# Retention and MoE kernel: two scalings moved to GpSimd, attention steps regrouped in the first GEMM2, and the last output tile copied by two engines

## The chip, the cores and the metric

The kernel runs on one core of one Trainium2 chip. The metric is the device time of one execution in microseconds (us); lower is better. The engines of the core are named as the profile names them: PE (TensorE, matmuls; PEld is its weight load), DVE (VectorE), ACT (ScalarE), POOL (GpSimd) and SP (SyncE, which here only issues DMAs).

## The reference

A causal retention layer (attention without softmax, with a decay per head) is followed by a two-layer network with a hardswish gate.

```python
# q, k, v: (8 batches, 8 heads, 576 positions, 64), w_in: (512, 2048), w_out: (2048, 512)
scores = scale * np.matmul(q, k.transpose(0, 1, 3, 2))
gamma = 1.0 - 2.0 ** (-5.0 - np.arange(H))
Dmat = np.where(rel >= 0, gamma[:, None, None] ** rel, 0.0)      # rel = pos[:, None] - pos[None, :]
attn = np.matmul(scores * Dmat, v)                               # x = attn as (4608, 512)
h = x @ w_in
g = h * np.clip(h + 3.0, 0.0, 6.0) / 6.0
out = g @ w_out                                                  # (4608, 512) float32
```

## The kernel before

**Pieces and blocks.** The 576 positions of a batch are cut into four pieces of 128 ("main") and a rest of 64; rests of two batches share a piece. Pieces 0 to 3 give the 512 tokens of block 0, pieces 4 to 7 those of block 1, and so on; block 8 holds all rests. For a piece the kernel loads K (`kn`) and Q with V (`qv`) from HBM through GpSimd's DMA queue (`load`, three DMAs each, with a cast to float16; six buffers), scales V, and in blocks from 2 on Q too, by the decay (`vs`), transposes K and Q (`qk`), forms scores, masks them (`at`), multiplies by V and adds what the state of earlier pieces contributes (`intra`, `inter`, `state_mm`); the result, cast, is the input `xt` of the network. `update_mm` and `update_state` carry the state on.

**Two ways to transpose.** For pieces 0 to 7, TensorE transposes K and Q into PSUM (`k_by_pe`, `q_by_pe`) and ScalarE copies them out. From piece 8 on, SyncE issues a transposing DMA for K (`transpose_k`) and, after Q and V have been scaled by one instruction over 128x1024, one for Q (`transpose_q`). `ahead(c)` does both for piece c.

**The network.** GEMM1 of a block is 16 units (`g1`) of four matmuls; ScalarE and VectorE form the gate (`gt`, lines 423 and 424). GEMM2 of block 0 is 16 units of four matmuls, (tile, part), `g2`; GEMM2 of later blocks uses seven products of half-size matrices (`product` 1 to 7, line 533) instead of eight. It needs differences of quarters of W_out (`combine_wout` 1 to 4, tiles `tw`) and sums of quarters of the gate (`sum_of`, tiles `s`, line 507). `gather` puts the products together and stores them.

**Order.** The order on each engine is written out by hand: instructions are issued engine by engine in the order of the program, and each waits for its own operands. `put(units, steps)` issues a list of units, and behind unit j the steps listed under j; `run_later` issues masks that were put off. In GEMM2 of block 0 the units go part by part over tiles 0 to 2, then tile 3. `first_step(c)` behind a unit finishes piece c-1, transposes piece c+1, forms the scores of piece c and scales V of piece c. In GEMM1 of block 1 the steps are the transposing DMAs and scalings of pieces 8 to 11. `seven_block(kb, mine, next_)` is GEMM2 of block kb with the attention of two blocks around it: pieces `mine` (c0 to c3) are finished, and the pieces `next_` (n0 to n3) are prepared. In block 1, `ahead(n0)` and `ahead(n1)` (pieces 12 and 13) stand behind product 2 and `gather(kb, 2)`; their scores come under `begin(n0, n1)`, just ahead of product 4.

**Resources.** PSUM has the tag `ph` with four banks (gates, units, transpositions), and `sc` (two banks), `tu` and `o` (one bank each).

Of the kernel before, what the change touches and what calls it, by code (L numbers as in the profile page):

```python
# [10 lines left out]
FP32 = mybir.dt.float32  # L11
FP16 = mybir.dt.float16
ACTF = mybir.ActivationFunctionType
ALU = mybir.AluOpType
# [3 lines left out]
def kernel(  # L18
# [16 lines left out]
    nc = tc.nc  # L35
# [3 lines left out]
    P = 128  # L39
# [50 lines left out]
    loaded = {}  # L90
# [144 lines left out]
            nc.tensor.transpose(pk[:, p, :], kn[:, 2 * p:2 * p + 2, :], ident16)  # L235
        nc.scalar.copy(qk_of(c)[:, 1], pk)

    def q_by_pe(c):
        q16, qk = loaded[c]["q16"], qk_of(c)
        pq = psum.tile([P, NPAIR, P], FP32, tag="ph", bufs=4, name=f"trq_{c}")  # L240
        for p in range(NPAIR):
            for h2 in range(2):
                r = slice(h2 * HALF, h2 * HALF + HALF)
                nc.tensor.matmul(pq[r, p, :], q16[:, 2 * p + h2, :], dq[:, 2 * p + h2, :],
                                 start=(p == 0), stop=(p == NPAIR - 1), skip_group_check=True)
        if c == EARLY - 1:
            for p in (0, 2):
                nc.scalar.copy(qk[:, 0, p:p + 2], pq[:, p:p + 2])
        else:
            nc.scalar.copy(qk[:, 0], pq)  # L250
# [54 lines left out]
    def transpose_k(c):  # L305
        nc.sync.dma_start_transpose(qk_of(c)[:, 1], loaded[c]["kn"].rearrange("s h d -> s (h d)"))

    def transpose_q(c):
        vs = work.tile([P, 2, H, D], FP16, tag="vs", bufs=6, name=f"vs_{c}")
        st[c]["vs"] = vs[:, 1]  # L310
        nc.vector.tensor_tensor(out=vs, in0=loaded[c]["qv"], in1=gqv, op=ALU.mult)  # L311
        nc.sync.dma_start_transpose(st[c]["qk"][:, 0], vs[:, 0].rearrange("s h d -> s (h d)"))

    def scores(c, late=9, given=False):
# [67 lines left out]
    def update_state(c):  # L382
        kind, b, i, _ = pieces[c]
        if kind == "rest":
            return
        u = st[c]["u"]
        scale = gc_b[1 if i == PER - 1 and b % 2 else 0]
        tag, bufs = ("tf", B) if i == PER - 1 else ("ts", 4)
        ts = work.tile([P, NPAIR, D], FP16, tag=tag, bufs=bufs, name=f"ts_{c}")
        if i == 0:  # L390
            nc.vector.tensor_tensor(out=ts, in0=u, in1=scale, op=ALU.mult)
        else:
            ta = work.tile([P, NPAIR, D], FP32, tag="ta", bufs=2, name=f"ta_{c}")
            nc.vector.tensor_tensor(out=ta, in0=u, in1=state_of[b], op=ALU.add)
            nc.vector.tensor_tensor(out=ts, in0=ta, in1=scale, op=ALU.mult)
            st[c].setdefault("before", state_of[b])
        state_of[b] = ts
# [162 lines left out]
    def last_block(kb):  # L560

        my = seven[kb] = {}
        for i, q1 in done_to[kb].items():
            sum_of(kb, i, q1, 8)

        def both(which):
            for tt in range(2):
                product(kb, which, tt)

        def keep(which):  # L570
            my[which] = work.tile([P, 2, half_n], FP32, tag=f"part{which}", bufs=1,
                                  name=f"part{which}_{kb}")
            for tt in range(2):
                nc.scalar.copy(my[which][:, tt], my["b"][tt])

        both(1)
        keep(1)
        both(2)
        gather(kb, 2)
        store_rest(0, 2, lo_n, my["lo"][:, :, lo_n], (nc.sync, nc.sync))  # L580
        sum_of(kb, 4, 0, 8)
        sum_of(kb, 3, 0, 8)
        both(5)
        gather(kb, 5)
        both(6)
        keep(6)
        both(3)
        ends = {name: work.tile([P, 2, half_n], FP32, tag=f"end{name}", bufs=1,
                                name=f"end{name}_{kb}") for name in ("c12", "c22", "c21")}
        nc.vector.tensor_tensor(out=ends["c12"], in0=my[6], in1=my["c_all"], op=ALU.add)  # L590
        store_rest(0, 2, hi_n, ends["c12"], (nc.sync, nc.sync))
        for tt in range(2):
            product(kb, 7, tt)
            nc.vector.tensor_tensor(out=ends["c22"][:, tt], in0=my[5][:, tt], in1=my["b"][tt],
                                    op=ALU.add)
        store_rest(2, 2, hi_n, ends["c22"], (nc.sync, nc.scalar))
        for tt in range(2):
            product(kb, 4, tt)
            nc.scalar.copy(ends["c21"][:, tt], my["b"][tt])
            store_rest(2 + tt, 1, lo_n, ends["c21"][:, tt:tt + 1], (nc.sync, nc.scalar))  # L600

    def store2(kb, i, src):
# [55 lines left out]
    def unit2(kb, mc, part):  # L658
        return lambda: g2(kb, mc, part)

    def first_step(c):


        old, new, b = c - 1 >= EARLY, c + 1 < 8, pieces[c - 1][1]
        if old:
            before = state_of.get(b)
            o = psum.tile([P, NPAIR, P], FP32, tag="o", name=f"o_{c - 1}")
            st[c - 1].update(o=o, first=True)
            copy = intra(c - 1, copy_later=True, more=before is not None)
            update_mm([c - 1])  # L670
            load_until(c - 1 + NBUF)
            update_state(c - 1)
        if new:
            q_by_pe(c + 1)
        if old and new:
            run_later(9)
        if EARLY <= c < 8:
            scores(c, 0)
        if old and before is not None:
            state_mm(o, before, st[c - 1]["qk"], slice(0, P), False, True)  # L680
        if new:
            k_by_pe(c + 1, "ph" if old else "tu")
        if old:
            copy()
        if c < 8:
            run_later(9)
        if EARLY <= c < 8:
            scale_v(c)

    def ahead(c):  # L690
        transpose_k(c)
        transpose_q(c)

    def scores_second(c, tags):

# [33 lines left out]
    def seven_block(kb, mine, next_):  # L729

        seven[kb] = {}
        c0, c1, c2, c3 = mine
        n0, n1, n2, n3 = next_ or [None] * 4

        def both(which):
            for tt in range(2):
                product(kb, which, tt)

        def begin(one, other, tags):
            update_mm([one, other])  # L740
            masks[one] = scores(one, given=True)
            masks[other] = scores_second(other, tags)

        def mask(c):
            masks.pop(c)()

        def done(*cs):
            for c in cs:
                loaded.pop(c)

        run_later(9)
        for i, q1 in done_to[kb].items():
            sum_of(kb, i, q1, 8)
        if kb == SEVEN:
            begin(c0, c1, ("ph", "ph"))
            load_until(c1 + NBUF)
        both(1)
        gather(kb, 1)
        if kb == SEVEN:
            mask(c0)  # L760
        update_state(c0)
        spread_state(c0)
        if kb == SEVEN:
            mask(c1)
        elif next_:
            ahead(n0)
            ahead(n1)
        both(2)
        if kb == SEVEN:
            update_state(c1)  # L770
        gather(kb, 2)
        if kb == SEVEN:
            ahead(n0)
            ahead(n1)
        else:
            update_state(c1)
        both(6)
        gather(kb, 6)
        inter(c0)
        inter(c1, "ph")  # L780
        intra(c0)
        intra(c1)
        spread_state(c1)
        begin(c2, c3, ("ph", "ph"))
        done(c0, c1)
        load_until(c3 + NBUF)
        sum_of(kb, 3, 0, 8)
        mask(c2)
        sum_of(kb, 4, 0, 8)
        both(5)  # L790
        gather(kb, 5)
        update_state(c2)
        spread_state(c2)
        mask(c3)
        both(7)
        gather(kb, 7)
        update_state(c3)
        both(3)
        gather(kb, 3)
        inter(c2, "ph")  # L800
        inter(c3, "ph")
        intra(c2)
        intra(c3)
        done(c2, c3)
        if next_:
            begin(n0, n1, ("ph", "o"))
            load_until(n1 + NBUF)
            ahead(n2)
            ahead(n3)
            mask(n0)  # L810
            mask(n1)
        both(4)
        gather(kb, 4)
# [7 lines left out]
    def gemm1(kb, steps, at_units):  # L821
# [8 lines left out]
        for j, (i, q0, q1) in zip(at_units, early_sums):  # L830
# [5 lines left out]

    load_until(EARLY - 1 + NBUF)
    gemm1(0, {9: [(fill_gq,)]}, ())
    order = [(mc, part) for part in range(4) for mc in range(3)] + [(3, part) for part in range(4)]
    steps = {3: [(first_step, 3)], 6: [(make_mask_rest,)], 9: [(first_step, 4)],  # L840
             11: [(first_step, 5)], 13: [(first_step, 6)],
             14: [(first_step, 7), (transpose_k, 8)], 15: [(transpose_k, 9)]}
    for j, i in zip((5, 6, 7, 8), (1, 2, 3, 4)):
        steps.setdefault(j, []).append((combine_wout, i))
    put([unit2(0, mc, part) for mc, part in order], steps)

# [6 lines left out]
    for fc, cols in ((2, done), (0, last), (1, last), (3, done), (2, last), (3, last)):  # L853
        g1_columns(1, fc, banks[fc], cols)
    gts.pop(0)


    gemm1(1, {0: [(transpose_q, 9)], 1: [(transpose_k, 10)],
              4: [(transpose_q, 10)], 5: [(transpose_k, 11)], 8: [(transpose_q, 11)]}, (2, 6))
    spare += tbd[0:PER - 1]  # L860
    for kb in range(1, NMB - 1):
        seven_block(kb, of_block(kb + 1), of_block(kb + 2))
# [33 lines left out]
```

## Time and profile before

| | |
|---|---|
| time, median of 3 runs | 300.46 us (298.76 to 301.93) |
| the profiled execution | 300.89 us, span of its instructions 299.1 us |
| PE busy | 286.1 us (96%) |
| DVE busy | 233.4 us (78%) |
| ACT busy | 181.4 us (61%) |
| POOL busy | 109.0 us (36%) |
| instructions | 6608 |

In the rows of the timeline the first number is the start in us from the first instruction, the second the length; then engine, line, operation, tiles written and read, and in brackets the idle time before it and what ended it. In rows of windows stand the stretch, its length, the busy time of PE, PEld, DVE, ACT and POOL with the number of instructions, the granted clock of TensorE as a share, the share of time that the DMA engines were in use (it can exceed 1, since waiting packets count) and GB/s. Rows of DMA issues end with the KB of one and the median us from issue to landing. A group of the page ends with busy time, mean ns of one, and idle time before it. A "q" behind an engine's name is its queue of DMA issues.

### The profile page before, as it was taken

The numbers are of one execution on the slowest core, as the hardware profiler recorded it, in microseconds if no ns is written. First come the engines' busy times: TensorE is split into PE (matmuls) and PEld (weight loads), VectorE is DVE, ScalarE is ACT, GpSimd is POOL, SyncE is SP. The second block draws the span as 40 slices with busy tenths as digits, with TensorE's granted clock in tenths as the row PEclk, the third lists the DMA queues.
The fourth block names the chain that finished last, engine by engine and source line by source line (L and its number), as shares of the span: only waits on it lengthen the run. The fifth ranks groups of instructions, "written<-read, shape, count | busy, mean of one in ns | idle before, by whom it ended". The sixth has DMA issues, their size and how long they took to land.

```text
span 299.1 us, 6608 instructions
## 1 busy us (share of the span) xinstructions
PE 286.1 (96%) x2646; PEld 185.7 (62%) x2646; DVE 233.4 (78%) x386; ACT 181.4 (61%) x311; POOL 109.0 (36%) x135
## 2 busy tenths in 40 slices
PE   7889998999969999999999999999999999999994
PEld 2644445547844488548854884488448844884583
DVE  4758656799965999699969996999699979637951
ACT  5558535585636856785677567755785577427720
POOL 8982567736770007501750175019720000000000
PEclk9999999999998999999999999999999999999998
DMA  9999999999999619991999299929992250011014
GB/s 71 149 184 206 189 162 216 168 122 150 141 202 154 94 37 145 169 149 35 160 153 148 42 154 151 148 39 127 156 177 52 77 139 0 2 72 70 3 35 106
DMA packets 153327, 35.56 MB, mean 119 GB/s; under 512 B 143568, under 2 KB 149200, under 8 KB 153296
## 3 DMA queue, kind: packets, MB, share of 16 engines
q0 software_dynamic: 117264, 18.36, 93.8%
q1 hardware_dynamic: 35728, 16.52, 28.5%
q8 instruction: 20, 0.33, 0.5%
q10 hardware_dynamic: 304, 0.26, 0.3%
q14 instruction: 11, 0.09, 0.1%
HBM read 36.70 MB, written 9.44 MB: 154 GB/s over the span
## 4 chain that ended last, share of the span: by engine, by line
PE 75%; DMA 11%; DVE 6%; POOL 4%; issue 1%; ACT 1%; ACTq 0%; DVEq 0%; POOLq 0%
PE ph L416 36%; PE b L533 17%; PE c L533 8%; DMA wout<-in_moe_w_out_dram 5%; PE a L533 4%; DMA win<-in_moe_w_in_dram 3%; PE o L353 3%; POOL qv L101 2%; DMA qk<-vs 2%; PE sc L321 1%; POOL kn L101 1%; DVE s L507 1%; DVE tw L492 1%; PE o L204 1%; DVE at L325 1%
## 5 line engine op out<-in xcount | busy, mean ns | idle before, releaser
L424 DVE SCALAR_TENSOR_TENSOR gt<-u,ph 128x512 f16<-128x512 f32 x144 | 97.4, 686 | 31.2 <-ACT u L423 29.2
L423 ACT ACTIVATE u<-ph,cb 128x512 f32<-128x512 f32 x144 | 98.6, 688 | 27.1 <-PE ph L416 26.4
L416 PE MATMUL ph<-xt,win 128*128 128x512 f16 x496 | 109.4, 382 | 0.5 <-ACT xt L287 0.4
L416 PEld LDWEIGHTS <-win 128*128 128x128 f16 x560 | 55.1, 98 | 65.7 <-issue 2.0
L101 POOL DMA_DIRECT2D kn<-in_k_dram x40 | 34.4, 867 | 97.9 <-PE u L377 91.1
L533 PEld LDWEIGHTS <-s 128*128 128x128 f16 x512 | 49.4, 98 | 6.5 <-DVE s L507 0.2
L533 PEld LDWEIGHTS <-gt 128*128 128x128 f16 x384 | 36.6, 98 | 7.6 <-DVE gt L424 1.1
L101 POOL DMA_DIRECT2D qv<-in_q_dram x40 | 34.4, 868 | 5.9 <-DMA wout<-in_moe_w_out_dram 3.4
L101 POOL DMA_DIRECT2D qv<-in_v_dram x40 | 34.7, 873 | 3.0 <-DMA wout<-in_moe_w_out_dram 1.6
L533 PE MATMUL b<-tw,s 128*128 128x256 f16 x256 | 30.6, 273 | 0.0
L359 ACT CAST xt<-o 128x512 f16<-128x512 f32 x31 | 17.0, 590 | 16.4 <-PE o L353 13.4
L325 DVE TENSOR_TENSOR at<-sc,mask_wide 128x1024 f16<-128x1024 f32 x19 | 23.2, 1222 | 1.7 <-PE sc L321 1.5
L507 DVE TENSOR_TENSOR s<-gt 128x512 f16<-128x512 f16 (+2 forms) x39 | 23.1, 591 | 0.3
L543 ACT COPY part<-b 128x512 f32<-128x512 f32 x14 | 8.2, 587 | 18.6 <-PE b L533 18.6
L311 DVE TENSOR_TENSOR vs<-qv,gqv 128x1024 f16<-128x1024 f16 x28 | 18.2, 685 | 0.0
L708 ACT CAST raw<-sc 128x512 f16<-128x512 f32 x28 | 15.1, 593 | 3.6 <-PE sc L702 3.4
L533 PE MATMUL b<-tw,gt 128*128 128x256 f16 x128 | 16.0, 280 | 0.0
L533 PE MATMUL b<-wout,gt 128*128 128x256 f16 x128 | 15.6, 273 | 0.0
L533 PE MATMUL c<-tw,s 128*128 128x256 f16 x128 | 15.4, 273 | 0.0
L533 PE MATMUL c<-wout,s 128*128 128x256 f16 x128 | 15.3, 273 | 0.0
L533 PE MATMUL a<-wout,gt 128*128 128x256 f16 x128 | 15.3, 273 | 0.0
L474 PE MATMUL pout<-wout,gt 128*128 128x512 f16 x64 | 14.8, 379 | 0.0
(93 smaller groups left out, 262.3 us busy)
## 6 DMA issues: line engine op xcount, KB each, us to landing
kn<-in_k_dram POOLq DMA_DIRECT2D x32, 128.0 KB, 7.1
qv<-in_q_dram POOLq DMA_DIRECT2D x32, 128.0 KB, 7.2
qv<-in_v_dram POOLq DMA_DIRECT2D x32, 128.0 KB, 7.2
out_dram<-olo SPq DMA_DIRECT2D x7, 512.0 KB, 4.5
out_dram<-ohi SPq DMA_DIRECT2D x7, 512.0 KB, 7.9
wout<-in_moe_w_out_dram POOLq DMA_DIRECT2D x4, 512.0 KB, 15.0
win<-in_moe_w_in_dram POOLq DMA_DIRECT2D x3, 512.0 KB, 10.1
out_dram<-osb SPq DMA_DIRECT2D x4, 256.0 KB, 5.6
```

Source lines behind the costliest of these rows:

```text
L101: nc.gpsimd.dma_start(dst[p0:p0 + n], src[b, :, s0:s0 + n, :].rearrange("h s d -> s h d"))
L311: nc.vector.tensor_tensor(out=vs, in0=loaded[c]["qv"], in1=gqv, op=ALU.mult)
L325: mask = lambda: nc.vector.tensor_tensor(out=at.rearrange("t a b s -> t (a b) s"), in0=sc.rearrange("t a b s -> t (a b) s"), in1=mask_b[pi ...
L353: nc.tensor.matmul(o[r, p, :], vs[:, 2 * p + h2, :], at[:, h2, p, :], start=(st[c]["first"] and p == 0), stop=(p == NPAIR - 1 and not more ...
L359: nc.scalar.copy(xt_of(kb)[:, :, g0:g0 + P], o)
L416: nc.tensor.matmul(ph, win16[:, dmc, P * fc:P * fc + P], xt_of(kb)[:, dmc, :], start=(dmc == 0), stop=(dmc == NCC - 1))
L423: nc.scalar.activation(u, ph, ACTF.Relu, bias=cb[:, 0:1], scale=1.0 / 6.0)
L424: nc.vector.scalar_tensor_tensor(out=gts[kb][:, fc, :], in0=u, scalar=1.0, in1=ph, op0=ALU.min, op1=ALU.mult)
L474: nc.tensor.matmul(pout, gt[:, fc, P * mc:P * mc + P], wout16[:, fc, :], start=(fc == 0), stop=(fc == NFC - 1))
L507: nc.vector.tensor_tensor(out=sm[i][:, q], in0=one, in1=other, op=op)
L533: nc.tensor.matmul(my[chain][tt], left[:, k, P * tt:P * tt + P], right[:, k, :], start=(first and (tt == 0 or apart) and k == 0), stop=(k ...
L708: nc.scalar.copy(raw[:, h2], banks[h2])
```

## The change

Three things are changed.

1. In GEMM2 of block 0, `first_step(3)` and `first_step(4)` transpose K ahead of Q, and Q into the bank `o` instead of one of `ph`. Scores, mask and scaling of piece 4 are a step of their own behind unit 7 (`masked(4)`, `scale_v(4)`); combinations 2, 3 and 4 of W_out come behind them, behind unit 8. `first_step(c)` scales V of piece c+1. The units of part 3 of tiles 0 to 2 come behind unit (3, 0).
2. `ahead(12)` and `ahead(13)` are steps of GEMM1 of block 1 and no longer stand in block 1's `seven_block`; their scalings are done by GpSimd. On GpSimd's queue these two instructions stand between the loads of piece 13 and those of piece 14.
3. The copy of the very last 128x256 tile is split into two halves of 128 columns, one by ScalarE and one by VectorE.

```diff
-    def q_by_pe(c):
+    def q_by_pe(c, tag="ph"):
         q16, qk = loaded[c]["q16"], qk_of(c)
-        pq = psum.tile([P, NPAIR, P], FP32, tag="ph", bufs=4, name=f"trq_{c}")
+        pq = psum.tile([P, NPAIR, P], FP32, tag=tag, bufs=4 if tag == "ph" else 1,
+                       name=f"trq_{c}")
...
-    def transpose_q(c):
+    def transpose_q(c, engine=nc.vector):
         vs = work.tile([P, 2, H, D], FP16, tag="vs", bufs=6, name=f"vs_{c}")
         st[c]["vs"] = vs[:, 1]
-        nc.vector.tensor_tensor(out=vs, in0=loaded[c]["qv"], in1=gqv, op=ALU.mult)
+        engine.tensor_tensor(out=vs, in0=loaded[c]["qv"], in1=gqv, op=ALU.mult)
...
         for tt in range(2):
             product(kb, 4, tt)
-            nc.scalar.copy(ends["c21"][:, tt], my["b"][tt])
+            if tt == 0:
+                nc.scalar.copy(ends["c21"][:, tt], my["b"][tt])
+            else:
+                nc.scalar.copy(ends["c21"][:, tt, 0:P], my["b"][tt][:, 0:P])
+                nc.vector.tensor_copy(ends["c21"][:, tt, P:2 * P], my["b"][tt][:, P:2 * P])
...
+    def masked(c):
+        scores(c, 0)
+        run_later(9)
+
     def first_step(c):
...
+        elif new:
+            k_by_pe(c + 1, "tu")
         if new:
-            q_by_pe(c + 1)
+            q_by_pe(c + 1, "ph" if old else "o")
         if old and new:
             run_later(9)
-        if EARLY <= c < 8:
+        if EARLY < c < 8:
             scores(c, 0)
...
-        if new:
-            k_by_pe(c + 1, "ph" if old else "tu")
+        if old and new:
+            k_by_pe(c + 1, "ph")
...
-        if EARLY <= c < 8:
-            scale_v(c)
+        if EARLY <= c < 7:
+            scale_v(c + 1)
 
-    def ahead(c):
+    def ahead(c, engine=nc.vector):
         transpose_k(c)
-        transpose_q(c)
+        transpose_q(c, engine)
...
         gather(kb, 2)
-        if kb == SEVEN:
-            ahead(n0)
-            ahead(n1)
-        else:
+        if kb > SEVEN:
             update_state(c1)
...
-    order = [(mc, part) for part in range(4) for mc in range(3)] + [(3, part) for part in range(4)]
-    steps = {3: [(first_step, 3)], 6: [(make_mask_rest,)], 9: [(first_step, 4)],
+    order = [(mc, part) for part in range(3) for mc in range(3)] + [(3, 0)]
+    order += [(mc, 3) for mc in range(3)] + [(3, part) for part in range(1, 4)]
+    steps = {3: [(first_step, 3)], 6: [(make_mask_rest,)],
+             7: [(masked, 4), (scale_v, 4)], 9: [(first_step, 4)],
              11: [(first_step, 5)], 13: [(first_step, 6)],
              14: [(first_step, 7), (transpose_k, 8)], 15: [(transpose_k, 9)]}
-    for j, i in zip((5, 6, 7, 8), (1, 2, 3, 4)):
+    for j, i in zip((5, 8, 8, 8), (1, 2, 3, 4)):
         steps.setdefault(j, []).append((combine_wout, i))
...
     gemm1(1, {0: [(transpose_q, 9)], 1: [(transpose_k, 10)],
-              4: [(transpose_q, 10)], 5: [(transpose_k, 11)], 8: [(transpose_q, 11)]}, (2, 6))
+              4: [(transpose_q, 10)], 5: [(transpose_k, 11)], 8: [(transpose_q, 11)],
+              10: [(ahead, 12, nc.gpsimd), (ahead, 13, nc.gpsimd)]}, (2, 6))
```

## The prediction

> **What bounds the kernel now.** I read the first two parts of the page first, then the chain of waits, then windows and the timeline around each place that the change touches.
>
> ```profile
> PE 286.1 (96%) x2646; PEld 185.7 (62%) x2646; DVE 233.4 (78%) x386; ACT 181.4 (61%) x311; POOL 109.0 (36%) x135
> DMA  9999999999999619991999299929992250011014
> ```
>
> TensorE is busy for 96% of the span, so there is little to win except where it waits or runs slowly. The DMA row shows that the transfer engines are full in the first 13 slices of 7.5 us (to about 97 us); that is where landing times decide.
>
> The chain of waits (start, length, what) shows three such places.
>
> ```profile
> 40.81 3.50 DVE tw L492 x3
> ...
> 80.12 6.96 DMA qk<-vs
> 87.21 0.40 PE sc L702 x8
> 87.61 2.49 PE b L533 x16
> 90.10 14.86 PE ph L416 x64
> ...
> 119.01 1.85 PE b L533 x16
> 120.86 13.81 PE ph L416 x64
> ...
> 295.26 0.37 ACT endc L599
> ```
>
> First, the combinations of W_out stand on the chain in GEMM2 of block 0. Second, in block 1 a transposing DMA of piece 13 (8 to 11 are of block 2, 12 and 13 of block 3) stands on it until 80.12 + 6.96 = 87.08. Third, the last copy. The timeline gives the longest waits of TensorE in the first two places, and the windows give their sum in the first:
>
> ```profile
> 42.28 0.41 PE L244 MATMUL trq<-dq,qv 128*64 128x128 f16 x8 [0.49 <-DMA qv<-in_q_dram]
> 45.83 0.41 PE L353 MATMUL o<-at,vs 128*64 128x128 f16 x8 [0.75 <-DVE vs L222]
> 87.21 0.40 PE L702 MATMUL sc<-qk 64*128 64x128 f16 x8 [2.88 <-DMA qk<-vs]
> 36.45:55.30 18.85, 17.25 (x191) 8.99 (x188) 11.58 (x16) 8.38 (x15) 13.03 (x15) 1.00 2.10 184
> 88.70:92.10 3.40, 3.40 (x14) 1.60 (x12) 0.70 (x1) 0.85 (x3) 0.74 (x1) 0.50 2.08 159
> ```
>
> In 36.45 to 55.30, TensorE (second number) works 17.25 of 18.85 us: 1.60 us of waits. Behind the wait of 2.88 us comes a second cost, the last row: for 3.4 us the granted clock (third number from the end) is 0.50. The chain prices it: product 4 and the 64 matmuls after it take 2.49 + 14.86 = 17.35 us there, and 1.85 + 13.81 = 15.66 us one block later. That is 1.69 us. The short waits of the first place cost no clock (1.00).
>
> **The change, part by part.** The profiled execution took 300.89 us (span 299.1 us and 1.8 us around it); the sum is made against that, and the median of the three runs is 0.43 us lower.
>
> *GEMM2 of block 0.* No instruction is added there. Scores, mask and scaling of piece 4 move from behind unit 9 to behind unit 7 and so ahead of three of the four combinations of W_out; V of pieces 5 to 7 is scaled one step earlier; unit (3, 0) comes before the three units of part 3, and in the first two steps K is transposed ahead of Q and Q into another bank, so that a bank is free for (3, 0). I lay the new order on the measured durations.
>
> ```profile
> 36.45 5.34 PE L474 MATMUL pout<-wout,gt 128*128 128x512 f16 x24
> 46.96 1.23 DVE L325 TENSOR_TENSOR at<-sc,mask_wide 128x1024 f16<-128x1024 f32 x1
> 48.10 0.41 DVE L222 TENSOR_TENSOR vs<-qv,gqv 128x512 f16<-128x512 f16 x1
> ```
>
> A unit of four matmuls takes 5.34 / 6 = 0.89 us. From 36.45, units 4 to 7 end at 40.0 and the scores of piece 4 at 40.3. VectorE, which until then waits for W_out, masks (1.23) and scales (0.41) until 42.0, and TensorE asks for both only at 44.5, behind units 8 to 11 and the transpositions of piece 5: the 0.75 us goes. Q of piece 5, which ends the wait of 0.49 at 42.28, is asked for at 42.45, since a unit and the K transposition now come first: that goes too. VectorE then does its three combinations (3.50) until 45.5, scaling 5, state 4, mask 5 until 47.4, where TensorE asks at 47.8; mask 6 ends at 50.4 and is asked for at 50.35, mask 7 at 53.1 for 53.8. So the margins are 2.5, 0.2, 0.4, -0.05 and 0.7 us: 1.5 of 1.6 us go, and TensorE enters GEMM1 of block 1 about 1.5 us earlier. Without that cover (VectorE 0.5 us later throughout) 0.5 us would stay. The stores of tiles 0 to 2 leave some 1.5 us later on SP's queue, ahead of transpositions that wait for their own loads. Bounds: -0.8 to -1.6.
>
> *Block 1.* Two scalings of 128x1024 leave VectorE and go to GpSimd, and the four transposing DMAs of pieces 12 and 13 are written into GEMM1 of block 1; their order on SP's queue stays. In before, the first waits for its turn on VectorE:
>
> ```profile
> 15.76 1.18 POOL L222 TENSOR_TENSOR vs<-qv,gqv 128x512 f16<-128x512 f16 x1
> 58.59 0.88 POOL L101 DMA_DIRECT2D qv<-in_v_dram  x1
> qv<-in_v_dram POOLq DMA_DIRECT2D x1, 128.0 KB, 10.0
> 61.37 0.90 POOL L101 DMA_DIRECT2D qv<-in_v_dram  x1
> qv<-in_v_dram POOLq DMA_DIRECT2D x1, 128.0 KB, 12.0
> 76.08 1.28 DVE L311 TENSOR_TENSOR vs<-qv,gqv 128x1024 f16<-128x1024 f16 x2
> DMA to landing us min/median/max: 5.6/7.4/9.5
> ```
>
> The one scaling by GpSimd took 1.18 us for 512 elements a row, so 2.36 for 1024. V of piece 12 is issued at 58.59 and lands 10.0 later (68.6), that of piece 13 at 61.37 and lands at 73.4. GpSimd scales 68.7 to 71.1 and 73.4 to 75.8. The Q transposition of piece 13 is then issued at 75.8 in place of 80.12, and with the 6.96 of the chain it lands at 82.8. TensorE wants it at 84.3 - 1.5 = 82.8. So the 2.88 us go, and with no long wait the slow clock goes too: -1.69. (The last row above is all transpositions between 49 and 92 us; 5.6 instead of 6.96 leaves a reserve.)
>
> New is that VectorE works while GpSimd computes on SBUF. These rows are of before:
>
> ```profile
> 16.00 0.69 DVE L264 TENSOR_TENSOR at<-sc,mask_wide 128x512 f16<-128x512 f32 x1 [0.37 <-PE sc L262]
> 69.19:84.34 15.15, 15.12 (x229) 13.02 (x228) 14.88 (x24) 8.76 (x18) 10.67 (x13) 1.00 2.21 147
> 70.74 0.69 DVE L507 TENSOR_TENSOR s<-gt 128x1024 f16<-128x1024 f16 x1
> 74.07 0.69 DVE L711 TENSOR_TENSOR at<-raw,mask_wide 128x1024 f16<-128x1024 f16 x1
> 79.55 1.22 DVE L507 TENSOR_TENSOR s<-gt,s 128x2048 f16<-128x2048 f16 x1
> 80.82 1.92 PE L533 MATMUL c<-wout,s 128*128 128x256 f16 x16
> ```
>
> VectorE is busy 14.88 of 15.15 us in this stretch, and the sum at 79.55 ends 0.05 us before product 3 (80.82) needs it. Lower bound: no hindrance; a mask next to GpSimd's scaling took its usual 0.69, but it reads PSUM. Upper bound: the engines take turns. The sum of 70.74, now due at 69.2, waits for 71.1 (1.9 us); the mask of 74.07, then due at 74.4, waits for 75.8 (1.3). Less the 1.28 that left VectorE, product 3 is 1.9 us late. No row decides between 0 and 1.9; I take the middle, +0.95.
>
> *What is queued behind.* GpSimd works in order, so the six loads of pieces 14 and 15 stand behind the second scaling:
>
> ```profile
> 74.15 0.92 POOL L101 DMA_DIRECT2D qv<-in_v_dram  x1
> qv<-in_v_dram POOLq DMA_DIRECT2D x1, 128.0 KB, 7.1
> qv<-in_q_dram POOLq DMA_DIRECT2D x1, 128.0 KB, 13.4
> qk<-vs SPq DMA_TRANSPOSE x1, 8.0
> ```
>
> The first leaves at 75.8, and the last, five issues of 0.88 later, at 80.2 instead of 74.15; with 7.1 it lands at 87.3. VectorE scales piece 15 behind that, then masks 12 and 13, then the first gate of GEMM1 of block 2: 0.64 + 1.23 + 0.69 + 0.69 and pauses, some 3.4 us, so 90.7. TensorE, past product 4 at 84.9 to 86.8 (by the bounds above), has four banks, 3.5 us (13.81 / 16 a unit), before it needs that gate: 88.4 to 90.3. That is 0.4 to 2.3 us of waiting with a landing of 7.1, nothing with two us less. GpSimd issued no load from 62.3 to 75.8, so fewer transfers compete than in before: I take +0.3. (The last two rows, a load at 87.65 and the Q transposition of piece 9, serve the rivals.)
>
> *Last tile.* In the instruction lists VectorE's half of the copy waits for ScalarE's half, so the two run one after the other.
>
> ```profile
> L543 ACT COPY part<-b 128x512 f32<-128x512 f32 x14 | 8.2, 587 | 18.6 <-PE b L533 18.6
> 293.07 0.42 DVE L594 TENSOR_TENSOR endc<-part,b 128x256 f32<-128x256 f32 x1 [0.45 <-PE b L533]
> ```
>
> ScalarE: 0.37 for 256 columns, 0.59 for 512, so about 0.26 for 128. VectorE: 0.42 for 256 columns, so between half of it and all, say 0.28. Together some 0.57 with the handover, against the 0.37 of the chain: +0.2 (bounds +0.1 to +0.35).
>
> Sum: -1.5 - 2.88 - 1.69 + 0.95 + 0.3 + 0.2 = -4.6; 300.89 - 4.6 = 296.3, and against the median 300.46 - 4.6 = **295.8 us**.
>
> **The rivals.** (1) The engines exclude each other in full: +1.9 instead of +0.95, and the late loads cost next to nothing since all is later: 300.46 - 1.5 - 2.88 - 1.69 + 1.9 + 0.2 = 296.5. For it: two instructions of 2.36 us fall into a stretch where VectorE has no slack. Against it: the one overlap in before shows nothing. The Trainium skill speaks for it ("SBUF — State Buffer", section "Who interferes with whom"): a VectorE instruction with two SBUF inputs and a GpSimd instruction that reads SBUF share a read port, and the second to start waits for the other to end; no run here shows it yet.
>
> (2) A wait takes the place of the one removed: the transposition of piece 13 needs 9.5 us, the longest of its kind, lands at 85.3, and TensorE still idles 2.5 us and loses its clock: 300.46 - 1.5 - 0.4 + 0.2 = 298.8.
>
> (3) GEMM2's gain does not arrive: the Q transposition of piece 9 takes 8.0 us to land, and scores at the start of block 1 wait for it. If the full transfer engines and not its issue set that landing, the 1.5 us comes back as a wait there: 297.3. For it speaks the DMA row, against it that nothing in the chain of before stands on that transposition.
>
> (4) Slower: the late loads of piece 15. If the last needs 13.4 us, the longest near there, it lands at 93.6, the first gate ends at 97.0, and the other 12 units (13.81 x 12 / 16 = 10.4) end at 107.4. The idle 8 us also bring the slow clock (1.7): 109.1, against 104.96 in before. That is +4.1 + 0.2: 304.8. It decides from a landing of about 9 us (89.2) on; for it speak the full transfer engines to 97 us, against it the pause in loads.
>
> **How the numbers follow.** Forecast 0.60, rival 1 0.17, rival 2 0.09, rival 3 0.07, rival 4 0.07. One per cent is 3.0 us, about what a measurement of this kernel can tell from no change: faster means below 297.5. Forecast, rival 1 and half of rival 3 lie there: 0.80; rival 2 and the rest of 3 are within: 0.13; rival 4: 0.07. Range: the low end takes every favourable bound, 300.46 - 1.6 - 2.88 - 1.69 + 0.1 = 294.4; the high end 298.6 takes in rival 1 with the weaker gain in GEMM2, rival 3 and almost rival 2.
>
> **What would show it.** Right: TensorE's waits between 36 and 54 us under 0.3 us; no wait before the scores of piece 13; granted clock 1.00 from 80 to 95; the last store some 0.2 us further behind the last matmul. For the hindrance: VectorE's sum or mask starts only as GpSimd's scaling ends, or takes longer than 0.69. Wrong: a wait over 1 us on a transposition or on the scaling of piece 15, or a stretch at 0.50 before 290 us.

## The result, and the profile after

The changed kernel takes 297.70 us (median of 20 runs, 296.16 to 301.24) against 299.92 us (20 runs, 297.64 to 302.21) for the kernel before: ratio 0.9934, 95% interval 0.9910 to 0.9958, or -2.2 us. The forecast was -4.6 us. Medians hold every execution; ratios and counts of executions leave out a few slow ones, and the profile of the changed kernel's second run, which was one of them (489.74 us, clock 0.56), is not read. On a second chip the changed kernel took 297.53 against 299.38 us, ratio 0.9917 [0.9883, 0.9951]. The direction is right and the size is half of what was predicted.

The profiled execution took 297.51 us with a span of 295.7 us, so the pair of profiles moved by -3.4 us: more than the medians, which is the first hint of what went wrong. The first part of the page after:

```profile
PE 285.9 (97%) x2646; PEld 186.0 (63%) x2646; DVE 234.6 (79%) x385; ACT 180.9 (61%) x311; POOL 113.2 (38%) x137
```

VectorE has lost two scalings, 1.28 us in all, and is nevertheless busier (233.4 to 234.6 us). The chain of waits after:

```profile
70.07 1.98 DVE s L508
...
74.76 1.75 DVE at L721
...
85.48 1.85 PE b L534 x16
87.34 13.81 PE ph L417 x64
```

The transposing DMA of piece 13 is gone from the chain, and product 4 with the 64 matmuls behind it takes 1.85 + 13.81 us, as in every later block. In their place stand two VectorE instructions of 1.98 and 1.75 us. The timeline of GpSimd and VectorE shows why they are so long:

```profile
69.37 2.12 POOL L312 TENSOR_TENSOR vs<-qv,gqv 128x1024 f16<-128x1024 f16 x1 [6.75 <-ACT u L424]
73.82 2.12 POOL L312 TENSOR_TENSOR vs<-qv,gqv 128x1024 f16<-128x1024 f16 x1 [2.33 <-DMA qv<-in_v_dram]
70.07 1.97 DVE L508 TENSOR_TENSOR s<-gt 128x1024 f16<-128x1024 f16 x1
73.21 1.22 DVE L326 TENSOR_TENSOR at<-sc,mask_wide 128x1024 f16<-128x1024 f32 x1
74.67 1.82 DVE L721 TENSOR_TENSOR at<-raw,mask_wide 128x1024 f16<-128x1024 f16 x1
```

The sum of 70.07 took 0.69 us before and 1.97 now: GpSimd's scaling ends at 71.49, and 71.49 + 0.69 is 72.18, close to where the sum ends (72.04). The mask of 74.67 ends at 76.49, 0.55 us behind the end of the second scaling (75.94). That is +1.28 and +1.13 us; less the 1.28 that left VectorE, 1.13 of the 1.61 us that this stage grew (below). The mask of 73.21, one of whose operands lies in PSUM, has its usual 1.22 beside GpSimd.

The windows, cut at the same five places in both kernels (start and end of GEMM2 of block 0, start of product 3, start of product 4, start of the products of the next block), put the whole difference into stages. The kernel before, then the kernel after:

```profile
32.32:54.07 21.75, 20.15 (x210) 10.37 (x209) 13.53 (x20) 8.64 (x16) 15.16 (x18) 1.00 2.01 189
54.07:80.82 26.75, 26.55 (x269) 17.60 (x267) 24.71 (x40) 18.36 (x31) 15.71 (x19) 1.00 2.33 145
80.82:87.55 6.73, 3.85 (x75) 3.28 (x73) 5.61 (x10) 1.89 (x4) 4.77 (x6) 1.00 2.08 155
87.55:104.80 17.25, 17.25 (x84) 8.38 (x82) 11.47 (x19) 11.96 (x18) 1.89 (x3) 0.90 1.29 146
```

```profile
32.98:53.40 20.42, 20.12 (x211) 10.56 (x209) 13.68 (x21) 8.43 (x16) 15.98 (x19) 1.00 2.01 188
53.40:81.76 28.36, 27.28 (x269) 17.70 (x268) 25.95 (x38) 18.50 (x31) 15.54 (x16) 1.00 1.91 138
81.76:85.42 3.66, 3.66 (x75) 3.23 (x72) 3.63 (x8) 1.73 (x4) 3.66 (x5) 1.00 2.38 152
85.42:100.99 15.57, 15.57 (x85) 7.81 (x81) 12.98 (x21) 12.04 (x19) 6.31 (x8) 1.00 1.80 185
```

Stage by stage: GEMM2 -1.33, up to product 3 +1.61, up to product 4 -3.07, product 4 and the 16 units behind it -1.68 (granted clock 0.90 to 1.00). The start of GEMM2 came 0.66 us later in this execution. The end of the span adds 0.42. First the last store of the kernel before, whose copy begins at 295.26, then the end of the kernel after:

```profile
295.67 0.50 ACTq L464 DMA_DIRECT2D out_dram<-endc  x1
```

```profile
291.44 0.27 ACT L603 COPY endc<-b 128x128 f32<-128x128 f32 x1 [0.58 <-PE b L534]
291.74 0.29 DVE L604 COPY endc<-b 128x128 f32<-128x128 f32 x1 [2.07 <-ACT endc L603]
292.06 0.50 ACTq L465 DMA_DIRECT2D out_dram<-endc  x1
```

The store is issued 0.62 us after the copy begins, against 0.41 with one copy, and from there to the end of the span it is 3.64 instead of 3.43 us. 0.66 - 1.33 + 1.61 - 3.07 - 1.68 + 0.42 = -3.4, the difference of the spans. Without the later start it is -4.05: for this pair most of the forecast arrives. What is to be found is why the medians move so much less.

### The profile page after: what moved, and what is told of

Read it like the earlier page. It is cut to its first block, busy times and chain, and to the rows that moved or that the text cites. A ratio compares the mean times of both kernels' runs of the same rounds, so it can differ in the third digit from the quotient of the medians.

```text
span 295.7 us, 6609 instructions
## 1 busy us (share of the span) xinstructions
PE 285.9 (97%) x2646; PEld 186.0 (63%) x2646; DVE 234.6 (79%) x385; ACT 180.9 (61%) x311; POOL 113.2 (38%) x137
## 4 chain that ended last, share of the span: by engine, by line
PE 90%; DVE 4%; ACT 2%; DMA 1%; issue 1%; POOL 0%; ACTq 0%; POOLq 0%
PE ph L417 41%; PE b L534 17%; PE c L534 10%; PE pout L475 5%; PE a L534 4%; PE o L354 3%; PE sc L322 2%; PE o L204 1%; DMA qv<-in_q_dram 1%; PE u L378 1%; DVE s L508 1%; PE sc L712 1%; PE trq L245 1%; PE ph L439 1%; PE trk L235 1%
## 5 line engine op out<-in xcount | busy, mean ns | idle before, releaser
L425 DVE SCALAR_TENSOR_TENSOR gt<-u,ph 128x512 f16<-128x512 f32 x144 | 97.4, 686 | 29.2 <-ACT u L424 27.1
L508 DVE TENSOR_TENSOR s<-gt 128x512 f16<-128x512 f16 (+2 forms) x39 | 24.3, 623 | 0.3
L312 DVE TENSOR_TENSOR vs<-qv,gqv 128x1024 f16<-128x1024 f16 x26 | 16.9, 684 | 0.0
L534 PE MATMUL b<-tw,gt 128*128 128x256 f16 x128 | 15.4, 273 | 0.0
```

Source lines behind the costliest of these rows:

```text
L312: engine.tensor_tensor(out=vs, in0=loaded[c]["qv"], in1=gqv, op=ALU.mult)
L425: nc.vector.scalar_tensor_tensor(out=gts[kb][:, fc, :], in0=u, scalar=1.0, in1=ph, op0=ALU.min, op1=ALU.mult)
L508: nc.vector.tensor_tensor(out=sm[i][:, q], in0=one, in1=other, op=op)
L534: nc.tensor.matmul(my[chain][tt], left[:, k, P * tt:P * tt + P], right[:, k, :], start=(first and (tt == 0 or apart) and k == 0), stop=(k ...
```

## The experiments

All ran with the kernel before on the same chip. "Stages" are the four of above.

**The kernel before, again**, and **its parts: GEMM2 of block 0 alone, block 1 alone**, and **the wait filled with matmuls**. The second and third kernel are the kernel before with the first or the second of the three changes; the last copy is as before. The fourth puts 13 matmuls of 512 columns on zeros ahead of the scores of piece 13:

```diff
             masks[one] = scores(one, given=True)
+            if other == 13:
+                warm(13, MBLK)
             masks[other] = scores_second(other, tags)
```

> The kernel before, once more, for a second profile and the clock of every execution. The pair of profiles differs by 3.4 us, the medians of many executions by 2.0 to 2.2. Theory: the stretch at half clock behind the wait of 2.88 us comes in a part of the executions of before only; then its executions fall into some with a mean granted clock near 0.991 and others near 0.997, about 1.7 us apart, and a new profile may show clock 1.00 behind the wait. Rival: the slow stretch comes in every execution and the two profiles were a lucky pair; then every execution shows 0.991 and about the same time. Ratio 1.000 either way.

> The part in GEMM2 of block 0 alone. Theory: 1.3 us of waits go there (as in the profile after), the wait for piece 13 stays near 2.9 us with its clock; ratio 0.9957. Rival (the full transfer engines set the landings, so what is won is waited for at the start of block 1 or before the scores of piece 13): that wait grows to 3.5 us or more and the ratio is 0.999 to 1.000.

> The two scalings on GpSimd and the four transposing DMAs ahead, alone. Theory: the wait of 2.88 us goes, about 1.4 us of it are given back where VectorE waits for GpSimd (its sum 1.3 us, its mask 1.1 us longer), and the half clock goes in those executions that had it: 1.5 us plus a share of 1.7, ratio 0.990 to 0.995. Rival (half clock in every execution of before): 3.2 us, ratio 0.989. Without any exclusion of the two engines: 0.985.

> The kernel before, with 13 matmuls on zeros (13 x 0.22 = 2.8 us) ahead of the scores of piece 13, so that TensorE is busy while it waits; the wait for the transposing DMA stays as it is. Every theory: granted clock 1.00 from 84 to 95 us, and product 4 with the 64 matmuls behind it back at 15.7 us from 17.35. Half clock in every execution of before: 1.7 us less, ratio 0.9943. In a part of them only: 0.996 to 0.999.

Measured, against 299.79 us for the kernel before: again 300.14 us, ratio 1.0021 [0.9989, 1.0053]; GEMM2 alone 299.07 us, 0.9982 [0.9946, 1.0019]; block 1 alone 296.74 us, 0.9906 [0.9871, 0.9941]; filled wait 299.25 us, 0.9989 [0.9960, 1.0018]. The part in GEMM2 can't be told from nothing, nor from the 0.9957 that was expected. Block 1 alone is, as far as the intervals tell, no worse than the whole change. Their windows, first two of GEMM2 alone, then three of block 1 alone:

```profile
33.51:53.93 20.42, 20.12 (x210) 10.56 (x209) 13.68 (x21) 8.42 (x16) 15.85 (x19) 1.00 2.04 188
80.68:86.45 5.77, 3.85 (x72) 3.27 (x72) 5.61 (x10) 1.88 (x4) 3.60 (x5) 1.00 2.20 163
```

```profile
33.15:53.53 20.38, 20.02 (x211) 10.39 (x210) 13.54 (x20) 8.45 (x16) 14.55 (x17) 1.00 2.00 190
53.53:80.09 26.56, 26.39 (x268) 17.71 (x267) 24.49 (x39) 18.36 (x31) 17.04 (x17) 1.00 1.88 148
80.09:83.75 3.66, 3.66 (x74) 3.22 (x72) 3.63 (x8) 1.72 (x4) 3.66 (x5) 1.00 2.31 147
```

Two things are to be seen. Block 1 alone has the old GEMM2, and yet its GEMM2 takes 20.38 us, as short as the new one: it started at 33.15 instead of 32.32, and a part of W_out on which VectorE waits had landed at 40.0 instead of 40.8. And its stage up to product 3 takes 26.56 us, not 28.36: the same two scalings by GpSimd are there, but they fell differently:

```profile
67.48 2.67 POOL L311 TENSOR_TENSOR vs<-qv,gqv 128x1024 f16<-128x1024 f16 x1 [6.43 <-DMA qv<-in_v_dram]
67.48 0.68 DVE L311 TENSOR_TENSOR vs<-qv,gqv 128x1024 f16<-128x1024 f16 x1
70.19 0.69 DVE L507 TENSOR_TENSOR s<-gt 128x1024 f16<-128x1024 f16 x1
73.52 1.31 DVE L711 TENSOR_TENSOR at<-raw,mask_wide 128x1024 f16<-128x1024 f16 x1
```

GpSimd's first scaling began 1.9 us sooner than in the profile after, since V of piece 12 had landed sooner (67.4 instead of 69.2). VectorE's own scaling of 67.48 was first, so GpSimd waited (2.67 instead of 2.12 us); it was done at 70.15, just before VectorE's sum. Only the mask was held, by 0.62 us.

The clock: with the wait filled it stays at 1.00 over product 4 and its 16 units.

```profile
87.30:102.87 15.57, 15.57 (x85) 7.83 (x82) 11.47 (x19) 11.94 (x18) 1.94 (x3) 1.00 1.42 159
```

And yet the ratio is 0.9989: a gain of some 0.3 us, at most 1.2 by the interval, where a half clock in every execution would have cost 1.7. Some of what is missing is taken by the filling itself: the transposition of piece 13 was issued at 79.64 and landed 7.0 us later, at 86.6, while the matmuls on zeros held TensorE until 87.0.

But the kernel before does not always lose it either. The waits ahead of the scores of piece 13, in the run again, in GEMM2 alone, and in an experiment told below (a late start of the kernel before), and behind them the windows of product 4 and the units for the first two:

```profile
87.25 0.40 PE L702 MATMUL sc<-qk 64*128 64x128 f16 x8 [2.78 <-DMA qk<-vs]
86.12 0.40 PE L708 MATMUL sc<-qk 64*128 64x128 f16 x8 [1.93 <-DMA qk<-vs]
86.42 0.40 PE L702 MATMUL sc<-qk 64*128 64x128 f16 x8 [2.02 <-DMA qk<-vs]
```

```profile
87.59:104.83 17.24, 17.24 (x83) 8.60 (x81) 11.46 (x19) 11.95 (x18) 2.00 (x3) 0.90 1.31 142
```

```profile
86.45:102.02 15.57, 15.57 (x83) 7.85 (x81) 11.46 (x19) 11.93 (x18) 2.86 (x4) 1.00 1.50 157
```

The half clock (0.90 on average) followed the first wait and the third (its window is shown further down), not the second. The mean granted clock of each run says more: one stretch of 3.4 us at 0.50 lowers it to 0.994. Of the 97 executions of the kernel before that are counted, 28 have 0.995 or more, so no full stretch; their median span is 296.6 us, that of the other 69 is 298.5. Of 28 executions of the changed kernel 19 have none, with 296.1 us, and the other 9 have 294.9; these are no longer, so their stretch presumably lies where it costs little: profiles of several variants show one near 10 us or behind the last matmul. The mean does not say where a stretch lies: with the wait filled, 8 of 12 executions are still below 0.995.

**The changed kernel again; GpSimd's scalings in halves; without them; the old last copy.**

```diff
-        engine.tensor_tensor(out=vs, in0=loaded[c]["qv"], in1=gqv, op=ALU.mult)
+        if engine is nc.gpsimd:
+            for half in range(2):
+                engine.tensor_tensor(out=vs[:, half], in0=loaded[c]["qv"][:, half],
+                                     in1=gqv[:, half], op=ALU.mult)
+        else:
+            engine.tensor_tensor(out=vs, in0=loaded[c]["qv"], in1=gqv, op=ALU.mult)
```

```diff
+        if engine is nc.gpsimd:
+            st[c]["vs"] = loaded[c]["qv"][:, 1]
+            nc.sync.dma_start_transpose(st[c]["qk"][:, 0],
+                                        loaded[c]["qv"][:, 0].rearrange("s h d -> s (h d)"))
+            return
```

The second of these edits leaves out the scaling of pieces 12 and 13.

> The changed kernel as it is, for a second profile and beside the other variants. Theory 1 (what the change is worth depends on how the landing of V of pieces 12 and 13 falls against VectorE's sums and masks): ratio 0.993 again, but the VectorE instruction that is held by a GpSimd scaling, and for how long, differs from the first profile; product 4 still starts without a wait, 0.5 to 2 us away from 85.4. Rival (the hindrance is fixed by the order of instructions): the same sum of 128x1024 at about 70.1 takes 1.97 us and the same mask 1.82 us again.

> The changed kernel, with each of GpSimd's two scalings as two instructions of 128x512. Theory 1 (a VectorE instruction with two SBUF operands waits for the one GpSimd instruction that runs): the held VectorE instructions wait at most 1.1 us and take at most 1.8, instead of 1.97 and 1.82 us on average 1.3; the kernel is 0.5 to 1.2 us faster than the changed one, ratio to the kernel before 0.990. Rival (VectorE waits until GpSimd has nothing left to do, or GpSimd's doubled overhead eats it): 1.9 us again, ratio 0.993.

> The changed kernel without the two scalings by GpSimd: Q of pieces 12 and 13 is transposed unscaled out of the buffer into which it was loaded, and V is used from there unscaled; the decay of these two pieces is left out. Theory 1 (the two instructions cost VectorE 1 to 2.4 us and nothing else on the path changes): product 3 comes 1 to 2 us earlier than with them and the kernel is 1 to 2 us faster than the changed one, ratio 0.987 to 0.990. Rival 2 (what the change gains in block 1 is limited elsewhere, by landing of the transposed Q): ratio 0.992 to 0.994, with a wait ahead of product 4 that takes the place.

> The changed kernel with the last copy by ScalarE alone, as in the kernel before. The profiles put the end of TensorE to the end of the span at 4.74 us with the two halves and at 4.3 us in every kernel with the whole copy. Theory 1 (the two halves run one after the other): 4.3 us here, the kernel 0.4 us faster than the changed one, ratio 0.992. Rival (the end is set by the store's landing, which varies): 4.3 to 4.8, no difference.

Measured, against 299.38 us for the kernel before: the changed kernel 297.53 us, ratio 0.9917 [0.9883, 0.9951]; halves 296.35 us, 0.9906 [0.9871, 0.9940]; without the scalings 295.96 us, 0.9899 [0.9864, 0.9934]; old copy 298.23 us, 0.9921 [0.9885, 0.9956]. The stage up to product 3 without the scalings, with halves, and with whole scalings again (the old copy):

```profile
55.17:81.66 26.49, 26.31 (x269) 17.65 (x267) 24.08 (x39) 18.48 (x32) 13.17 (x16) 1.00 1.93 149
53.07:80.16 27.09, 26.52 (x269) 17.50 (x268) 24.73 (x39) 18.33 (x31) 17.93 (x19) 1.00 1.97 151
55.52:83.41 27.89, 26.92 (x268) 17.58 (x267) 25.59 (x38) 18.32 (x31) 17.34 (x17) 1.00 1.87 136
```

26.49, 27.09 and 27.89 us, beside 28.36 in the profile after: the two instructions on GpSimd cost the path 1.4 to 1.9 us, and halves take back part of it. The run times show this less clearly: the ratios 0.9917 and 0.9899 differ by some 0.5 us, their intervals overlap, and the medians of the executions behind them (297.21 and 295.96 us) differ by 1.2. The timeline with halves shows who waits for whom:

```profile
69.62 1.15 POOL L314 TENSOR_TENSOR vs<-qv,gqv 128x512 f16<-128x512 f16 x1 [0.85 <-DMA qv<-in_q_dram]
71.50 2.10 POOL L314 TENSOR_TENSOR vs<-qv,gqv 128x512 f16<-128x512 f16 x1 [0.72 <-DMA qv<-in_v_dram]
69.74 1.58 DVE L513 TENSOR_TENSOR s<-gt 128x1024 f16<-128x1024 f16 x1
71.36 1.23 DVE L513 TENSOR_TENSOR s<-s,gt 128x2048 f16<-128x2048 f16 x1
73.96 0.69 DVE L726 TENSOR_TENSOR at<-raw,mask_wide 128x1024 f16<-128x1024 f16 x1
```

The sum of 69.74 waits for one half of 1.15 us. The next sum, at 71.36, starts first, and now GpSimd's half waits (2.10 instead of 1.15); the mask is free. Between these two halves GpSimd was idle for 0.72 us, so they do not tell a lock by instruction from "VectorE waits until GpSimd has nothing left to do". A later run with halves, block 1 alone, does, since there two halves follow each other at once:

```profile
67.46 2.71 POOL L313 TENSOR_TENSOR vs<-qv,gqv 128x512 f16<-128x512 f16 x2 [5.58 <-DMA qv<-in_q_dram]
67.53 1.62 DVE L316 TENSOR_TENSOR vs<-qv,gqv 128x1024 f16<-128x1024 f16 x1
```

VectorE's scaling is held by the first half and ends at 69.15, 1.02 us before GpSimd's second half does (70.17). So that rival falls. With the old copy it is 4.3 us from the end of TensorE to the end of the span (292.62 to 296.9), as expected; in the run times that doesn't show, the interval of the ratio holds both.

**A late start.** The start varies. In the profiles without the scalings and with the old copy GEMM2 began as late as 34.75 and 35.10 us, since a stretch of half clock lay at the start of GEMM1 of block 0 (another lay near 10 us in both); with the old copy:

```profile
20.00:22.00 2.00, 1.93 (x5) 0.71 (x5) 0.00 (x0) 0.29 (x2) 2.00 (x3) 0.50 1.24 207
```

Product 4 stood at 87.55, 87.59 and 87.30 in three profiles of kernels with the old block 1, whose GEMM2 began at 32.32, 33.11 and 32.71: as if TensorE had no say in it (in the fourth, GEMM2 alone, it stood at 86.45, with a start at 33.51). Hence a test, with eight matmuls on zeros ahead of GEMM1 of block 0, in both kernels:

```diff
+    warm(8, MBLK)
     gemm1(0, {9: [(fill_gq,)]}, ())
```

> The kernel before with eight matmuls of 512 columns on zeros ahead of GEMM1 of block 0 (1.7 us of TensorE). Theory 1 (in the kernel before, product 4 of block 1 is set by when V of piece 13 lands, whatever TensorE did until then): the first GEMM2 starts 1.4 to 1.7 us later (34.0 to 34.8), product 4 still starts at 87.3 to 88.0, and the ratio is 0.998 to 1.002. Rival (what is lost at the start is lost at the end): product 4 at 89, ratio 1.005.

> The changed kernel with the same eight matmuls ahead of GEMM1 of block 0. Theory 1 (the changed kernel has no wait left ahead of product 4, so that TensorE's own work sets it): the first GEMM2 and product 4 both start 1.4 to 1.7 us later, less what GpSimd's scalings then hold VectorE less; ratio to the kernel before 0.995 to 0.998, so that with a late start nearly all of the change's gain is gone. Rival (landings set product 4 here too): ratio 0.992 as without them.

Measured, against 299.56 us: the kernel before with a late start 1.0000 [0.9963, 1.0037]; the changed kernel with a late start 299.02 us, 0.9983 [0.9947, 1.0019]. Windows of the kernel before, then of the changed one, both with the late start:

```profile
33.77:54.14 20.37, 20.01 (x210) 10.37 (x209) 13.56 (x20) 8.45 (x16) 14.61 (x18) 1.00 2.01 188
54.14:80.89 26.75, 26.48 (x270) 17.57 (x267) 24.70 (x40) 18.32 (x31) 15.40 (x18) 1.00 2.22 150
80.89:86.75 5.86, 3.84 (x72) 3.27 (x73) 5.61 (x10) 1.88 (x4) 3.70 (x5) 1.00 2.16 160
86.75:103.99 17.24, 17.24 (x84) 8.64 (x82) 11.47 (x19) 11.94 (x18) 2.76 (x4) 0.90 1.41 144
```

```profile
33.82:54.24 20.42, 20.12 (x211) 10.57 (x209) 13.68 (x21) 8.43 (x16) 15.98 (x19) 1.00 2.05 186
54.24:82.24 28.00, 26.92 (x268) 17.61 (x267) 25.69 (x38) 18.33 (x31) 18.32 (x19) 1.00 1.96 146
82.24:85.90 3.66, 3.66 (x74) 3.23 (x72) 3.63 (x8) 1.72 (x4) 1.76 (x3) 1.00 3.19 146
```

The kernel before starts GEMM2 1.45 us later than in its first profile and ends it at 54.14 instead of 54.07: the delay takes the place of its waits there. What VectorE, and behind it TensorE, waited for there is a transfer of W_out; in the first profile of the kernel before:

```profile
40.81 1.23 DVE L492 TENSOR_TENSOR tw<-wout,tw 128x2048 f16<-128x2048 f16 x1 [5.49 <-DMA wout<-in_moe_w_out_dram]
```

With the late start this instruction begins at 40.51, hardly moved. The start alone does not decide: six profiles with the old GEMM2, begun at 32.32, 32.50, 32.71, 33.11, 33.15 and 33.77, took 21.75, 21.07, 21.15, 21.11, 20.38 and 20.37 us, and the new one took 20.42 wherever it began. Product 4 comes at 86.75, half a us sooner than the expectation's 87.3, not later. That a late start costs the kernel before nothing held. The changed kernel has no such wait, and with 1.7 us more work at the start its ratio is 0.9983, beside 0.9934 and 0.9917 without; the intervals overlap a little. In these two profiles the change brings +0.05 in GEMM2, +1.25 up to product 3 and -2.20 up to product 4.

**Towards a better version**: halves with the old copy, and block 1 alone with halves.

> The changed kernel with GpSimd's scalings in halves and the last copy by ScalarE alone. Theory 1 (the two costs add): product 3 stands 27.1 us or less behind the end of the first GEMM2 (28.4 and 27.9 in the two profiles with whole scalings), TensorE's end stands 4.3 us before the end of the span, and the ratio is 0.989 to 0.990, faster than the changed kernel and the kernel before. Rival (halves helped by chance of the landings): 0.992.

> Only the part of the change in block 1, with GpSimd's scalings in halves; GEMM2 of block 0 and the last copy as before. Theory 1 (the part in GEMM2 of block 0 is worth 0.5 to 1 us on top of this one): ratio 0.991 to 0.993, 0.5 to 1 us slower than the variant with it. Rival (the part in GEMM2 gives nothing that arrives): the same ratio as the variant with it, 0.989 to 0.990.

Measured, against 299.56 us: 296.37 us, 0.9885 [0.9828, 0.9942], and 296.24 us, 0.9887 [0.9840, 0.9933], six executions each. The stage up to product 3 took 27.35 us (27.1 or less was expected) and 27.30.

Both beat the kernel before, and by their ratios the changed kernel (0.9917 and 0.9934); they were not timed beside it on one chip, and the intervals overlap. They can't be told apart, so no gain of the part in GEMM2 shows. The simpler one, block 1 alone with halves, is the version that I would keep.

## Why the prediction was right in direction and wrong in size

**The step that failed** is the sum. It took the price of two waits and of one slow stretch from a single execution and charged them in full to the median: -1.5 for GEMM2, where the run with that part alone gave some -0.5 (not told from nothing), and -1.69 for the clock, which not every execution of the kernel before loses. And it put GpSimd's hindrance at +0.95, where the stage grew by 1.1 to 1.6 us.

**The waits.** Right for the wait of 2.88 us: no wait stands before the scores of piece 13 in any kernel with the new block 1 (3.66 us between products 3 and 4 in the profiles of the changed kernel and of block 1 alone). TensorE's waits in GEMM2 fell to 20.42 - 20.12 = 0.30 us, as forecast. The granted clock was 1.00 from 80 to 95 us.

**The late loads** were put at +0.3 and cost nothing: rival 4 fell. The six transfers landed 4.4 to 4.5 us after their issue, not 7.1:

```profile
qv<-in_v_dram POOLq DMA_DIRECT2D x2, 128.0 KB, 4.5
```

**The transposition of piece 9** (rival 3) cost nothing either: from the end of GEMM2 to 70 us the one wait of TensorE that is longer than 0.1 us is one of 0.18 for a gate.

**The last tile** was serial as forecast, but at twice the price: +0.42 instead of +0.2, since the store, too, took 0.2 us longer to the end.

**The hindrance was one term that failed.** The prediction took the middle between none and taking turns, on the ground of one overlap with a mask that reads PSUM, and put rival 1 at 0.17. In every overlap read here, the engines take turns when both operands of VectorE's instruction lie in SBUF: 1.1 to 1.6 us net up to product 3 with whole scalings (26.75 to 27.89, 28.00 and 28.36), instead of +0.95; in block 1 alone, where only the mask was held, nothing net (26.56). The Trainium skill, "SBUF — State Buffer", section "Who interferes with whom", states such a lock for a VectorE instruction with two SBUF inputs beside a GpSimd instruction that reads SBUF, and that the order of issue decides who waits. The traces agree on both: sum 0.69 to 1.97 us behind GpSimd, GpSimd 2.12 to 2.67 us behind VectorE. The one overlap that spoke against it was of an instruction with an operand in PSUM, which is just the case that is spared (1.22 us at 73.21, beside GpSimd). The prediction's credit was off too: it took off all of the 1.28 us that left VectorE, but without the scalings, and so without any hold, the stage takes 26.49 us, only 0.26 less than the 26.75 before, with TensorE busy for 26.31 of it.

**The second failure is larger: terms of one execution were charged to the median.** The sum was made against a profiled execution that had an early start (GEMM2 at 32.32, the earliest of all profiles), the longest GEMM2 and the longest wait for piece 13, and a stretch of half clock. Two terms hang on that. The -1.69 of the clock was real in that pair (-1.68), but 28 of 97 executions of the kernel before have no full stretch, so at most 0.7 of it, some 1.2 us, can be charged on average, and the filled wait gave 0.3, of which the filling itself hides some more. And the -1.5 in GEMM2 was there in that pair (-1.33), but is +0.05 when the start is late: behind those waits stands a landing of W_out (and, for 0.49 us, one of Q), and that of W_out hardly moved when TensorE did. GEMM2 alone gave 0.9982, or -0.5 us. The prediction read the waits as VectorE's, behind W_out, and never asked what they would be if the start moved.

With what the runs showed, the sum for a middling execution is: GEMM2 -0.5, wait -2.1 to -3.1, clock -0.3 to -1.2, hindrance +1.1 to +1.6, loads 0, copy +0.4: between -0.9 and -3.3, beside -2.2 and -1.9 measured. In executions without a full stretch the two kernels differ by 0.5 us (296.6 to 296.1). That could mean that most of the gain is the clock, and that GpSimd's lock and the copy give back nearly all that the wait had cost. But executions of the kernel before that keep their clock may be those that waited least (of the profiles with the old block 1 and no filling, the one that kept it, GEMM2 alone, waited only 1.93 us), and filling the wait gained only some 0.3. How the gain divides between wait and clock is not shown.

What stays open, beside that division: why GpSimd's scalings fall on VectorE's sum in all three profiles with both parts and whole scalings, and beside it in that of block 1 alone. What else they hold differs: in the profile after it is the mask, in those of the changed kernel with the old copy and with the late start it is VectorE's own scaling (1.48 and 1.43 us instead of 0.68), and there the mask is free. So the hold is not fixed by the order of instructions alone. Landing of V of piece 13 varies from 70.6 to 73.7 us between the profiles, so a difference of chance can't be excluded.

## What to carry to other kernels

A term that is a wait for a transfer belongs to the execution in which it was seen: ask how it changes when the start moves by a microsecond, and test it by delaying the start, which costs one line. Work that is moved to GpSimd is not free for VectorE; look at where VectorE's operands lie, cut GpSimd's instructions short, or put them beside instructions that read PSUM. And a slow clock that one profile shows is a chance, to be weighed by how many executions have it; a mean clock counts such stretches, but does not say where they lie.

## What the runs showed of the hardware

The lock between VectorE and GpSimd goes both ways (sum 0.69 to 1.97 us; GpSimd's 128x512 half 1.15 to 2.10 us) and is by instruction (VectorE's scaling ran to its end between two halves of GpSimd's, at 69.15). Two halves on GpSimd cost hardly more than the whole (2 x 1.15 against 2.12 us).

The clock fell to 0.50 behind waits of 2.02, 2.78 and 2.88 us, and not behind one of 1.93; the stretch behind each of the three was one of 3.4 us. Four waits do not tell a threshold near 2 us from chance. The Trainium skill, "TensorE: Matmul & The Clock Gate", advises in "Why this matters for your kernels" against gaps of over about 3 us, and describes a free-running window in "What's actually happening". A free-running window would fit executions with and without; but here gaps below 3 us were enough, and no trace here shows where a window begins.
